# Linear attention and a gated mixture of attention experts on one core: the same steps in another listed order

## The chip, the core and the metric

The kernel runs on one core of a Trainium2 chip, in one launch. The metric is the device time of an execution in microseconds (us), the median of three runs. A core has a matrix engine (TensorE, PE in the profile; its weight loads stand under PEld), VectorE (DVE), ScalarE (ACT) and GpSimd (POOL), each with its own queue in order, and SyncE (SP), whose queue issues most of the loads and stores. SBUF is the core's working memory of 128 partitions; matmuls write to PSUM, of which this kernel uses eight banks of 128 x 512 elements.

## The reference

```python
def phi(x):
    proj = np.einsum('bhsd,df->bhsf', x, w_phi)
    proj = proj - np.max(np.abs(proj), axis=-1, keepdims=True)
    return np.concatenate([np.exp(proj), np.exp(-proj)], axis=-1)
q_p, k_p = (phi(q), phi(k))
kv = np.einsum('bhsf,bhsd->bhfd', k_p, v)
z = np.sum(k_p, axis=2)
num = np.einsum('bhsf,bhfd->bhsd', q_p, kv)
den = np.einsum('bhsf,bhf->bhs', q_p, z)[..., None] + 1e-06
x = num / den                     # then (batch, 576, 512), heads side by side
...
logits = x @ w_gate               # 4 experts, the best 2 of each row weighted by a softmax
for e in range(4):
    q, k, v = x @ wq[e], x @ wk[e], x @ wv[e]
    a = softmax(0.125 * q @ k.T, causal)
    out += weight_e * (a @ v @ wo[e])
```

There are 8 batches of 8 heads, 576 rows, 64 columns a head and 128 features. The second part is a causal attention of 576 rows for each batch and expert.

## The kernel before, in words

The work is cut into steps. Generators stand for streams: loads of k, q and v (`load_k`, `load_q`, `load_v`), projections of keys and queries of the 32 pairs of heads (`stream_k`, `stream_q`, matmuls of L499), their features (`phi_k`, `phi_q`), the sums over keys (`stream_kv`: L591 and L599 for the last 64 rows, L624 for kv, L635 for z), numerators and denominators (`stream_n`: L721 and L732), and for each batch the projections (L295), scores (L852), gates (`gates`), row maxima (`maxima`), sums of scores (`sums`, L1019), weighted values (L1048) and the output projection (L295 again). A step that copies from PSUM may go to ScalarE (L304) or to VectorE (L316).

Matmuls use the array in shapes: 128x128 (L295, L646), 64x128 (L499, L852), 64x64 (a part of L852), 64x32 (L591, L599) and 128x32 (L624, L635, L721, L732, L1019, L1048, L942).

The order is written out. `ORDER` (L72) is a string with one character a step: it names the place, in the list of live streams, of the stream that takes its next step. `SIDES` (L104) has one digit for each step that may go to either of two engines, 0 for ScalarE and 1 for VectorE. `Plan.loop` (L226) reads both:

```python
for c in ORDER:
    s = self.streams[ord(c) - 48]
    st = s[1]
    assert st.pred is None or st.pred()
    if isinstance(st.eng, tuple):
        st.eng = st.eng[int(next(sides))]
```

A step issues its instructions when it is taken, so this one string sets the order in every engine's queue, in SP's queue of loads and in GpSimd's. A step that needs a PSUM bank takes the free bank that was last used earliest. `in_order` (L246) ties each instruction to the one before it on its engine, and lets each GpSimd reduction or mask (L694, L977, L960) wait for the last VectorE operation listed ahead of it that works in SBUF alone.

Three helpers matter here. `phi_q` (L689) has GpSimd find the largest absolute value over 128 partitions (L694, `mx` from `u`), which VectorE then subtracts (L696). `maxima` (L963) does the same for scores (L977), and VectorE subtracts it from the scores (L981). `key_sum` (L570) has GpSimd issue a transfer that adds in SBUF (L332, from `ek` to `zs`, 512 KB), after which VectorE adds two halves (L574) and TensorE sums them (L635). `keep_warm` (L457) issues rounds of three small matmuls on a tile `warm` at the start until the first row block of x is there.

Of the kernel before, what the change touches and what calls it, by code (L numbers as in the profile page):

```python
# [69 lines left out]


ORDER = (  # L72
    r'10000030084C0009CD9247DC26FBGB98BB0935E708GFG=HDB84DCH010HKDJGGHB0G0BG2EE=990=CBI5=BBD=7B::JE>2DHCC:4463=7988B'
    r'B=GGBJDD9::EGEE=>ELD=IH5:>21BJJEDE>HGD99=CCGHICFEB=G7J:H:ABH5425468FJ<IIE<0A<C;E@<<BFDGGF@EA;6DEEBFD@D7A;0HDE7'
    r'7JEDEDG6H9;;D99B8:F@B979G9C>AGFE99808E17A:?2AF@59H3CIJ6CEFB99LCL0IHFFJFG::H4>>>>96877D9FJ=EB8@FBBIBB=GBGB>8B6?'
    r'>EA;;5;;FGF;JDD@EAF?88E3=F012;C88:ECEDD8@6;5;=>B=?B8BBB999AEDID7BA6EBD=IHDA7;GH8DFC@;;;6IDJ;@H;HMJIHHB;EG;CCB?'
    r'FFFFGCFB18H08038F48G88;5HAGFAA=;;:CL>?8CCECBAAKCBB@:::B:9AGJC<EHG99HFF=A?DDDIEJ@BCC883228888D::I6P88GFKHINBF83'
    r'NGMA@77?NA5FE31?I@CKFD<99>>9KK<=KAKC8884820HKEKFI=E8GHA6=<DE987FF>B976G7>7I88I=<E=DAHD2<88888=5J9GALC<032KHBBJ'
    r'HA8?6L<LK0IKGBAF899=@77=H==BKDA:::<JJIOF>:N<<DIFAIIH::CLMDIIKH8;HEJJ;CEH:CI:LGC6;GF8H:IL5FKG8:::KGL@OQPN88IO::'
    r':MMM?J=M:A>L>AIK4MMKIKFFF?J882K>IJ=JE0IEE;G;HF<DE<<G?FHFGF=F@IC<:8M8;:5BGGIDHHCDFJEE<8IICHIC=BLIKMDHMC::JPOI:9'  # L80
    r'MPO<GRHHBFFPPP999JH6<D18EEGAF8J>FC<7F0CEIE@D38DFD83@@KCC@I>GG8BBHF;;BIH<E7C>CFG2DE8BBD?C==8DC>88B>==9;9=97KI7L'
    r'JI=F=FF8B5OG68OEOGB>E8888KLA9BL9M79F?LAGIKM8JJ54IJAIHJ8H6H<38=1@82887?G=BFB::::EJ6F:MDK=DEFAK:J<?F@8806C@??ACD'
    r'FF:AFGF988897GF?DAEDA>CDC7@@GDE2:G:C5KG:B@DCB8M@:J=EOA::N:088834230?IFHJFJI@I:IF=:H?GG=I=ABECD;98I88;EGH6E=AGG'
    r'EBED8D6C::DC::HCC:EDLGGIMMM<CDJ<@<KBBS=<<O?DNA9AFKRDOC;HEG99JDCBFJ?GAABI<K=J?883E??EG?E7GFF@GHG@FB@F79F=9H1ACM'
    r'CAGG<E5D888HAG2CAFF7I7888=@3>IDFF8D<E<8EEF<8<BCE<>G56889M>PQ8DCJHN8K>LLK>HK99;D9;IJ0JGHJD8GI@GG?EEEGF8E577:HK<'
    r'FFE<FH6FE>0::::8D88142C8M6EC?<CDEDG@K::FLHDA8893IBF@9EJFJ8AHE>D8FF87HF7I:CGJFDGDB:L::K:5LHJFAAGQ6@I>GF8JF=MMHI'
    r'K>A88D:EE:JE=AAF;:08==EI@D@@CGC8<ECGG8;;9JG8EE8DH:CIFFE>=H><G:<:5BEH:DCGF:>O6OE:<<HB2HGD@ANK<9A=KO@IP<M06GO93C'
    r'A1842883MF9EDBMHM888>88MIIH8KEK>AG9989IG=A8FJH8K7F78LL7L6HH8C>PHIQ=NHGCFKF23AKG8999NIE;H?K7B<HH5B=7IAHEEMJG4EI'
    r'I708IAE@:GG>DB<D8FB:B::NNG66:KFLL::K3@B8210828588KH9BJJILI=CABD9G78GJ7IJ6AF=B8HJ8LAMFGGLH=5<K<KJA8J==L=JA==E<D'
    r'DQIHO83880<P<<<;NHS;:BSHHGN8O8HMKN8NHHA:>:D:G=KGPFOB?OO:OKHLLIGGA:@NG:::;8<EKGNM6I?>MJKH>?FF;6K=IIIHGF;:FGFF8:'  # L90
    r'=I:9LCKEAB::FKLLFCD5JTE<RRRIDLFD<ETB<QQ10C4<DCNDCHEGCGC=MJCD<0QLQMHBF@EHCJ@9FE<9823GD88F@@I@HCC@GB88E<E888BECD'
    r'?HB;98HC<><>7@EBFABF5F76FEEELHF99481H@EIH>J@>@@DGHH9J6@FC6IF;;77KHN<LIH83J8888GEF989<HF8F<288@839@GG@HFCFH077K'
    r'JBI>CA28A<H858CCC<68:II::B:NELHHIJIACCHID:6IICE:89HE98FF5HC?GFGF@BFFGF7=::KJJG::M::LIKELPHH7H8F<FCNC<<>OOGOO0H'
    r'GFHJ:::;8:8F?J8?@MJ??KL>DDDH2=38GJGCDFDFF;;88;5FFH8<HKLKBHCB>CC6<EF<=@@DFDCH<C<BB:=??D?9EDFFFCJF::?FJGHEIIHH:G'
    r':AAEPG9NUD=NF9=C?FKF9G7QPD1737016NPMJNPDOPN?AF?77ICCE>?LDD16055GI5?J9H;<<?=AB5@<=A=AE3<2<E?666555GF=FD<50DHI:G'
    r'C<G;E;FE:9851?BB7558D?D@A54A2>AB@A4??4A3C12?A?>=2C==2C244EE6<222D654446I@BEH4=>=CF0007607020=CFDCD?0224459:=<0'
    r'B22A9=H112>I>@AF<ID080=C224C220@E9@>?0B88577<06:?7<:>59<:19::69:>99B?=8A9:2>3=0>:395;<:<7:9777445444085?=>=0<<'
    r'2<52;>7C6C99916@611000022?0@?87559A3A=5?3@C8=58:84:;;00<656670=888?6@88<7>;;=7=9:0;;6<<03<<9628488366442223:30'
    r'0000052258;;5:<32811:78:7796301000:2997:0>@55855509896598001005:7:;68757577;57515766655315005005846440:3B5@;5?'
    r'3;:=<1:8751715::2146464755444151211411143463311048518832223=;63229883717100817555667055651210010<=413<<<0<00::'  # L100
    r'52912855552200543010'
)

SIDES = (  # L104
    r'10000000111000000000000011000010000011000011000000010000000000000100100100000001000000000010000000000000000000'
    r'00000000010000001100000100000000000000000000000000000000000000000100001001000000000000110000000000000000000000'
    r'00001000000000000000010100000010100010000100000101000000110000000100000000000000010000001000010000000001000000'
    r'00010010110000000000101001000000000000000000000000010000001000110000000000011000000000011100000000100110101010'
    r'00100000100000000000000011000000000000010000000100000000001000000000000010110101'
)  # L110


# [1060 lines left out]
```

## Time and profile before

| | |
|---|---|
| median of 3 runs | 599.58 us (599.35 to 599.69) |
| the profiled execution | 600.02 us |
| its span, first to last instruction | 598.2 us |
| busy: TensorE, VectorE, ScalarE, GpSimd | 582.6, 542.5, 452.0, 276.9 us |

The span is the profiled execution's own time without what lies around the first and the last instruction, 1.8 us. A busy time is the time in which at least one instruction of that engine ran. Matmuls overlap each other, so a busy TensorE need not be one at its peak.

### The profile page before, as it was taken

To read this page: it belongs to the slowest core of one execution; us is meant where nothing else is said; L and a number is where in the kernel's file an instruction comes from. 1 tells how busy PE (TensorE), PEld (TensorE's weight loads), DVE (VectorE), ACT (ScalarE), POOL (GpSimd) and SP (SyncE) were. 2 spreads that over 40 slices of the span, in tenths; PEclk is the share of its full clock that TensorE was granted. 3 is DMA by queue.
4 is the path that set the end of the run, shared out by engine and by line. 5 is a ranking of instruction groups with operands and counts; after the bars stand their busy time and mean duration, and the time that the engine had idled before them with its cause. 6 is when DMAs were issued, how large, how long until landed. Compare 5 with 4: busy or idle time off the path is not lost.

```text
span 598.2 us, 19532 instructions
## 1 busy us (share of the span) xinstructions
PE 582.6 (97%) x7909; PEld 448.3 (75%) x7909; DVE 542.5 (91%) x1155; ACT 452.0 (76%) x1104; POOL 276.9 (46%) x195
## 2 busy tenths in 40 slices
PE   8999999999999999999899999999999999999986
PEld 6665888578875788767686787975887678778875
DVE  6899999899999989889799989999999999997894
ACT  4999969877798978868578668776879777677552
POOL 3564661186535484265521457407553746231420
PEclk9999999999999999999999999999999999999999
DMA  8758255663065572355446552446325643111013
GB/s 210 187 151 182 49 125 139 151 136 84 28 159 129 125 183 60 109 118 159 110 105 149 112 138 84 115 110 171 109 45 119 161 101 88 29 55 41 1 42 118
DMA packets 55369, 67.13 MB, mean 112 GB/s; under 512 B 23664, under 2 KB 31216, under 8 KB 55280
## 3 DMA queue, kind: packets, MB, share of 16 engines
q1 hardware_dynamic: 47344, 50.62, 29.6%
q0 software_dynamic: 7616, 14.68, 14.7%
q8 instruction: 62, 1.02, 0.7%
q10 hardware_dynamic: 320, 0.59, 0.4%
q14 instruction: 27, 0.22, 0.1%
HBM read 36.64 MB, written 14.55 MB: 86 GB/s over the span
## 4 chain that ended last, share of the span: by engine, by line
PE 75%; DVE 14%; ACT 4%; DMA 3%; issue 2%; POOL 1%; SPq 1%; ACTq 0%; DVEq 0%; POOLq 0%
PE ps_c L295 28%; PE ps_c L499 11%; PE ps_c L732 9%; PE ps_c L624 7%; PE ps_c L852 5%; PE ps_c L721 4%; PE ps_c L1048 4%; DVE s L981 2%; DVE top L973 2%; DVE max L993 2%; PE ps_c L591 1%; PE ps_c L635 1%; DMA q_in<-in_qt_dram 1%; DVE pmax L562 1%; DVE u L696 1%
## 5 line engine op out<-in xcount | busy, mean ns | idle before, releaser
L694 POOL PARTITION_ALL_REDUCE mx<-u x64 | 147.5, 2336 | 71.8 <-ACT u L304 14.2
L295 PE MATMUL ps_c<-x,qk 128*128 128x256 f32 (+1 forms) x768 | 107.6, 299 | 1.5 <-DVE ek L565 1.3
L295 PEld LDWEIGHTS ps_c<-x,qk 128*128 128x128 f32 x768 | 102.9, 190 | 6.4 <-issue 1.7
L960 POOL TENSOR_SCALAR_AFFINE_SELECT s<-s 128x256 f32<-128x256 f32 (+1 forms) x80 | 42.5, 562 | 94.3 <-ACT s L304 17.9
L977 POOL PARTITION_ALL_REDUCE max<-top x16 | 57.4, 3590 | 56.2 <-DVE top L973 19.3
L306 ACT ACTIVATE ek<-ek 128x1024 f32<-128x1024 f32 x64 | 67.8, 1059 | 5.5 <-DVE ek L565 4.8
L332 POOL DMA_DIRECT2D zs<-ek x28 | 34.3, 1224 | 75.5 <-DVE pmax L562 15.6
L981 DVE TENSOR_TENSOR s<-s,max 128x1152 f32<-128x1152 f32 (+4 forms) x80 | 66.6, 867 | 1.5 <-POOL max L977 1.4
L306 ACT ACTIVATE s<-s 128x640 f32<-128x640 f32 (+4 forms) x80 | 57.2, 739 | 6.4 <-DVE s L981 6.1
L624 PE MATMUL ps_c<-ek,v_in 128*32 128x256 f32 x1024 | 61.7, 381 | 0.0
L304 ACT COPY s<-ps_c 128x320 f32<-128x320 f32 (+4 forms) x140 | 52.6, 432 | 10.9 <-PE ps_c L852 10.2
L304 ACT COPY u<-ps_c 128x320 f32<-128x320 f32 (+1 forms) x110 | 40.4, 401 | 18.3 <-PE ps_c L499 18.0
L295 PE MATMUL ps_c<-yh,wo 128*128 128x320 f32 (+1 forms) x256 | 52.9, 300 | 0.0
L295 PE MATMUL ps_c<-vg,x 128*128 128x260 f32 x384 | 49.8, 289 | 0.2 <-DVE ql L805 0.2
L696 DVE TENSOR_TENSOR u<-u,mx 128x576 f32<-128x576 f32 x64 | 50.0, 793 | 0.0
L295 PEld LDWEIGHTS ps_c<-vg,x 128*128 128x128 f32 x384 | 48.0, 192 | 1.0 <-DVE ql L805 0.4
L624 PEld LDWEIGHTS ps_c<-ek,v_in 128*32 128x32 f32 x1024 | 31.5, 110 | 21.8 <-issue 2.2
L562 DVE TENSOR_REDUCE pmax<-ps_c 128x4 f32<-128x512 f32 x64 | 42.7, 676 | 5.5 <-PE ps_c L499 5.1
L306 ACT ACTIVATE mx<-u 128x576 f32<-128x576 f32 x64 | 43.1, 683 | 5.9 <-DVE u L696 5.7
L1048 PE MATMUL ps_c<-s,vs 128*32 128x320 f32 (+4 forms) x896 | 47.1, 357 | 0.0
L499 PE MATMUL ps_c<-q_in,wf 64*128 64x256 f32 (+1 forms) x256 | 44.0, 436 | 1.0 <-DMA q_in<-in_qt_dram 1.0
L732 PE MATMUL ps_c<-mx,kv 128*32 128x320 f32 (+1 forms) x512 | 43.4, 410 | 0.5 <-ACT u L304 0.3
(131 smaller groups left out, 1334.1 us busy)
## 6 DMA issues: line engine op xcount, KB each, us to landing
zs<-ek POOLq DMA_DIRECT2D x28, 512.0 KB, 6.2
out_dram<-ot SPq DMA_DIRECT2D x32, 288.0 KB, 2.2
q_in<-in_qt_dram SPq DMA_DIRECT2D x60, 144.0 KB, 3.9
k_in<-in_kt_dram SPq DMA_DIRECT2D x64, 128.0 KB, 3.9
v_in<-in_v_dram SPq DMA_DIRECT2D x32, 256.0 KB, 3.6
kvd<-kvt SPq DMA_DIRECT2D x104, 48.0 KB, 2.0
kv<-kvd SPq DMA_DIRECT2D x26, 192.0 KB, 2.8
vt_in<-in_v_dram SPq DMA_DIRECT2D x16, 128.0 KB, 3.4
```

Source lines behind the costliest of these rows:

```text
L295: nc.tensor.matmul(o, a, b, start=start, stop=stop, skip_group_check=True)
L304: nc.scalar.copy(o, i)
L306: nc.scalar.activation(o, i, func, **kw)
L499: nc.tensor.matmul(o, a, b, start=True, stop=True, skip_group_check=True)
L562: dve(512, [mk], [pk]).tensor_reduce(out=m[:, us], in_=src, axis=AX.X, op=ALU.max, apply_absolute_value=True)
L624: nc.tensor.matmul(o[g, 0:2], v_in[:, 4 * h + t, k:64:2], ek[:, :, 2 * TURN[t] + h, :].rearrange("p c (w f) -> p c w f", w=4), start=False ...
L694: nc.gpsimd.partition_all_reduce(M, U, 128, bass_isa.ReduceOp.absmax)
L696: dve(S, [uk], [mk], port=True).tensor_tensor(out=U, in0=U, in1=M, op=ALU.subtract)
L732: nc.tensor.matmul(ps[g:g + 32, 0:n], kvi[:, 2 * k + (h ^ p % 2), 32 * c:32 * c + 32], P_[h][c][:, s0:s1], start=c == 0, stop=c == 1, skip ...
L977: nc.gpsimd.partition_all_reduce(big.rearrange("p e s -> p (e s)"), top.rearrange("p e s -> p (e s)"), 128, bass_isa.ReduceOp.max)
L981: dve(2 * (S - 128 * j), [('d', x, j)], [('max', z)], 1.11, True).tensor_tensor(out=block(s_, j, None, rows(j)), in0=block(s_, j, None, ro ...
L1048: nc.tensor.matmul(ps[r:r + 32, q0 - s0:s1 - s0], vs[:, j, 128 * g + 64 * e + k:128 * g + 64 * e + 64:2], ss[x][:, e, o + q0:o + s1], star ...
```

## The change

`ORDER` and `SIDES` are other strings; not a line of code is different. The new list has three steps fewer, all three rounds of warm-up matmuls. The same transfers, tiles and other instructions are issued, in another order on every engine, and some copies from PSUM are on the other of their two engines.

```diff
 ORDER = (
-    r'10000030084C0009CD9247DC26FBGB98BB0935E708GFG=HDB84DCH010HKDJGGHB0G0BG2EE=990=CBI5=BBD=7B::JE>2DHCC:4463=7988B'
...
+    r'11030400000008929424D7FCBCCECC00EFE09BDE653E507E9CD8HHEG8D99D2KD=D=8BFG2EG4:=K7JFM==GKLJ:64BDECBEH=BBB97EFF8BD'
...
 SIDES = (
-    r'10000000111000000000000011000010000011000011000000010000000000000100100100000001000000000010000000000000000000'
...
+    r'10000100000110001010010000000000000100000101000010011000000000100000011100000001000000000000000000000000000000'
...
```

**First listing.** TensorE, early in the program, around the sum over z (L635, from `zs`) of a pair of heads. `ps_c` are PSUM banks. Before:

```order
L599 MATMUL ps_c_63<-ekt,ones 32x4x32
L624 MATMUL ps_c_67<-ek_108,v_in_106 32x2x4x32 x16
L635 MATMUL ps_c_67<-zs,ones 32x4x32 x4
L499 MATMUL ps_c_69<-q_in_104,wf 128x320
L499 MATMUL ps_c_66<-q_in_104,wf 128x320
L721 MATMUL ps_c_65<-mx_139,kv_119 32x288
L721 MATMUL ps_c_65<-mx_140,kv_119 32x288
```

and in the change:

```order
L599 MATMUL ps_c_66<-ekt,ones 32x4x32
L624 MATMUL ps_c_67<-ek_108,v_in_106 32x2x4x32 x16
L635 MATMUL ps_c_67<-zs,ones 32x4x32 x4
L721 MATMUL ps_c_65<-mx_139,kv_119 32x288
L721 MATMUL ps_c_65<-mx_140,kv_119 32x288
```

Before, two projections (L499, 64x128) stand between the sum over z and the denominators (L721, from `mx` and `kv`), which have the same shape, 128x32. In the change the denominators follow at once.

**Second listing.** VectorE, where the row maxima of a block of scores (`s`, `max`) are subtracted (L981). GpSimd's steps stand in the same written list: before, a transfer L332 ahead of the first row here, and one reduction L694 each ahead of the fourth, the sixth and the seventh row; in the change the transfer just ahead of the first row's step, and three reductions in one go ahead of the fourth row (the first L562). Before:

```order
L299 TENSOR_TENSOR x_146<-ps_c_65,x_146 128x256
L316 CAST yh_171<-ps_c_70 128x256
L765 TENSOR_TENSOR ps_c_68<-ps_c_68,xf 128x320
L299 TENSOR_TENSOR yl_172<-ps_c_70,yh_171 128x256
L981 TENSOR_TENSOR s_154<-s_154,max_156 128x2x576
L299 TENSOR_TENSOR x_146<-ps_c_68,x_146 128x320
L981 TENSOR_TENSOR s_154<-s_154,max_156 128x2x448
L562 TENSOR_REDUCE pmax_123<-ps_c_63 128x4
L565 TENSOR_TENSOR ek_109<-ps_c_63,pmax_123 128x4x128
```

and in the change:

```order
L765 TENSOR_TENSOR ps_c_63<-ps_c_63,xf 128x320
L696 TENSOR_TENSOR u_130<-u_130,mx_138 128x576
L299 TENSOR_TENSOR x_146<-ps_c_63,x_146 128x320
L562 TENSOR_REDUCE pmax_123<-ps_c_66 128x4
L565 TENSOR_TENSOR ek_109<-ps_c_66,pmax_123 128x4x128
L316 COPY u_131<-ps_c_68 128x256
L752 RECIPROCAL facd_163<-facd_163 128x18
L981 TENSOR_TENSOR s_154<-s_154,max_156 128x2x576
L562 TENSOR_REDUCE pmax_123<-ps_c_70 128x4
L565 TENSOR_TENSOR ek_109<-ps_c_70,pmax_123 128x4x128
```

L981 of 128x2x576 was listed right behind the last part of an output's evacuation (`yl`), between two reductions on GpSimd. Now a maximum and a subtraction for the keys' features (`pmax`, `ek`), a copy of `u` and a reciprocal stand between the reductions and L981.

**Third listing.** VectorE in the last batch, behind the subtractions of one block's maxima (L981) and ahead of the gates (from L915 on). `top` holds the running maxima (L973) that the last GpSimd reduction reads; L993 are the sums of the block before. Before:

```order
L316 COPY s_154<-ps_c_66 128x448
L316 COPY s_154<-ps_c_66 64x64
L993 TENSOR_TENSOR max_156<-s_153 128x2x448
L993 TENSOR_TENSOR max_156<-max_156,s_153 128x2x320
L973 TENSOR_TENSOR top_155<-s_154 128x2x448
L993 TENSOR_TENSOR max_156<-max_156,s_153 128x2x192
L973 TENSOR_TENSOR top_155<-top_155,s_154 128x2x320
L993 TENSOR_TENSOR max_156<-max_156,s_153 64x2x64
L973 TENSOR_TENSOR top_155<-top_155,s_154 128x2x192
L973 TENSOR_TENSOR top_155<-top_155,s_154 64x2x64
L743 STREAM_TRANSPOSE widey_142<-ps_c_70 128x288
L316 COPY vs<-ps_c_67 128x260
```

and in the change:

```order
L316 COPY s_154<-ps_c_68 128x256
L993 TENSOR_TENSOR max_156<-s_153 128x2x448
L993 TENSOR_TENSOR max_156<-max_156,s_153 128x2x320
L993 TENSOR_TENSOR max_156<-max_156,s_153 128x2x192
L973 TENSOR_TENSOR top_155<-s_154 128x2x448
L993 TENSOR_TENSOR max_156<-max_156,s_153 64x2x64
L973 TENSOR_TENSOR top_155<-top_155,s_154 128x2x320
L973 TENSOR_TENSOR top_155<-top_155,s_154 128x2x192
L973 TENSOR_TENSOR top_155<-top_155,s_154 64x2x64
L299 TENSOR_TENSOR yl_174<-ps_c_63,yh_173 128x320
L743 STREAM_TRANSPOSE widey_142<-ps_c_64 128x288
L829 TENSOR_TENSOR vs<-ps_c_65,vs 64x260
```

The two copies of scores (`s_154`, 448 columns and 64 rows of 64) have become one of 256 columns, and the copy of `vs` is no longer there; ScalarE has these copies now.

## Rows read from the trace of the kernel before

**Rows 1.** The page of the kernel before, span and part 1, and the clock by core.

```profile
span 598.2 us, 19532 instructions
PE 582.6 (97%) x7909; PEld 448.3 (75%) x7909; DVE 542.5 (91%) x1155; ACT 452.0 (76%) x1104; POOL 276.9 (46%) x195
...
core 0: 598.2 us, clock 0.997
```

**Rows 2.** The page, part 4: the chain that ended last, shares of the span.

```profile
PE 75%; DVE 14%; ACT 4%; DMA 3%; issue 2%; POOL 1%; SPq 1%; ACTq 0%; DVEq 0%; POOLq 0%
```

**Rows 3.** TensorE's waits: line, what ended them; us in total, times, longest.

```profile
PE ps_c L635 <- DVE zs L574: 1.8, 1, 1.8
PE ps_c L1019 <- DVE max L993: 1.5, 2, 1.2
PE ps_c L295 <- DVE ek L565: 1.3, 1, 1.3
...
PE ps_c L499 <- DMA q_in<-in_qt_dram: 1.0, 1, 1.0
...
PE ps_c L721 <- DMA kv<-kvd: 0.6, 1, 0.6
```

**Rows 4.** Timeline of TensorE, the end: start, us, instruction, [idle before <-releaser].

```profile
583.24 0.40 PE L1019 MATMUL ps_c<-max,ones 128*32 128x224 f32 x4 [1.20 <-DVE max L993]
...
593.31 0.31 PE L295 MATMUL ps_c<-yl,wo 128*128 128x320 f32 x1
```

**Rows 5.** Timeline of TensorE, the start.

```profile
1.06 2.10 PE L295 MATMUL ps_c<-warm 128*128 128x128 bf16 x18 [1.06 <-DVE col L339]
4.00 0.80 PE L499 MATMUL ps_c<-wf,kt_in 64*128 64x128 f32 x4 [0.84 <-DMA kt_in<-in_kt_dram]
```

**Rows 6.** The chain in order of time, two stretches: start, us, what.

```profile
54.62 2.08 PE ps_c L732 x32
56.70 1.73 PE ps_c L624 x32
...
319.36 2.18 PE ps_c L499 x15
321.54 1.87 PE ps_c L624 x32
```

**Rows 7.** Timeline of GpSimd and VectorE: a reduction beside L755, and L755 alone.

```profile
441.85 2.15 POOL L694 PARTITION_ALL_REDUCE mx<-u  x1 [4.99 <-DVE facy L752]
441.89 1.29 DVE L755 TENSOR_TENSOR facy<-facy,gc 128x18 f32<-128x18 f32 x1
...
292.84 0.17 DVE L755 TENSOR_TENSOR facy<-facy,gc 128x18 f32<-128x18 f32 x1
```

**Rows 8.** Timeline around 415 us, and L981 by form (xcount | busy, mean ns).

```profile
411.48 1.23 POOL L332 DMA_DIRECT2D zs<-ek  x1 [0.47 <-ACT ek L306]
412.25 7.08 POOL L694 PARTITION_ALL_REDUCE mx<-u  x3
...
412.19 3.02 DVE L981 TENSOR_TENSOR s<-s,max 128x1152 f32<-128x1152 f32 x1
...
418.69 0.41 PE L295 MATMUL ps_c<-x,qk 128*128 128x320 f32 x1 [1.33 <-DVE ek L565]
...
L981 DVE TENSOR_TENSOR s<-s,max 128x1152 f32<-128x1152 f32 x16 | 23.1, 1443 | 1.5 <-POOL max L977 1.4
```

**Rows 9.** Groups by form: xcount | busy us, mean ns of one | idle before, releaser.

```profile
L562 DVE TENSOR_REDUCE pmax<-ps_c 128x4 f32<-128x512 f32 x64 | 42.7, 676 | 5.5 <-PE ps_c L499 5.1
L316 DVE COPY u<-ps_c 128x256 f32<-128x256 f32 x7 | 2.8, 406 | 1.5 <-PE ps_c L499 1.5
...
L306 ACT ACTIVATE ek<-ek 128x1024 f32<-128x1024 f32 x64 | 67.8, 1059 | 5.5 <-DVE ek L565 4.8
```

**Rows 10.** The z transfers: duration ns min/median/max, first to last start; time to landing.

```profile
L332 POOL DMA_DIRECT2D zs<-ek x28: 1200/1220/1369, 42.5 to 505.0; - x28
...
DMA to landing us min/median/max: 5.1/6.2/7.4
```

More of the change, by code (lines that the diff above doesn't have):

```diff
@@ L78 @@
[L78 to L82, printed above, removed]
@@ new lines @@
+    r'9B=C>=8EFE=5KE:JFIGCI>>F:DB>:IHHHG9D=:B=HJEI:9BHG2G=HG378C:GHGG540;;C@D1<<<A@E;::9EE5IFHBC6HEE8DGGG4D;DAEK@GH;'
+    r'A7;<<AF:F7G@298;GC:CC::;EGEF9:CCCA30E::88FBB116F9>AHE7EC>>D?>>HGDH@E@DE4::3C9>B78E@8753:E9@0GB9421BBBCIHCBBCCB'
+    r'0C5E;;8;;=;HI;;8J?@F>IHCECD8=@A9FC>>CB886DDCBC8CD5;C9EADEABB=8D=C97F7AFH0IGG=;C;AA;HE>688A832J;JH>;I;;;GE88JFI'
+    r'H=FEBEEAABF?EG8DFFE@D;;5:C?D;?43L0A8@DA:=ED:DHAE@F@F@F@::::<HG6:?A999E8882308AQCBFDGD18?CNO8KFAMB688LKELABFLF8'
+    r'KHKIH@@HAH99@@<7EHBF56GF7>>481I888089E2=H==3CEBIE8=D=GG77KIH=AAG?=FC9988?95882HJA7876B=?MMK?FMGKL@HA288HEE86FL'
@@ new lines @@
+    r'?FLEE<IA99LKEGJIDI<H877><43<J>GIG<<IAD=:EII:F::::GJ8DKMLJ@<;AG;KAH8HC:::F?EOKK::KIHALLLFF5=J8QFFQ?>ALKEHMK::JG'
+    r'88I288::JHJJI:;@KFF1IIF0IGL?>K=>@L?G6D;;LHIH<<EHG<@KDDDF>EC88H::5=GGDBBHEEEGBBGB<BB<EFANJFJ?F?A:;BGB8=GDHII::9'
+    r'HDBTKIMGJGCJNNN9@GJ699BEEMGBB@@@ED?DHDFCCCB@HEBBAA088803FE@HE888;;I3C=D<FF8FF=8AC@C899=7>87=888DDD;7I2=HGC=E5='
+    r'BD7M9MC<68HII<8MOOHGK<J@@I@C99DMBNC798NO7NDLCC=JDIID6EJG?601324888:5D@D3KL:<::F::CMFMJEMKLIE@J88G8HJ8F6AJGII88'
+    r'C8HB9G9HHHH:7G7CHGI?H::NKC:JM:CBMC:EALG@ML5PIJJI:K::KBEAJH:JKBFH88813?6BG;J:;G=248C88GF@BKLIJ>FFH2D>AFE9@E>E8E'
@@ new lines @@
+    r':F8D:C::@FIEFMLFLKBABBBBJ<<D<<C>FLICKPK?OC<MH>DKKLJC999F0773<8BDD<GHDG?MKEE8HI<088?GHACD8G?6?KG@@JJFJ9B9JEBBEC'
+    r'@HJ75NLC<CBIJ8AHF=G?8H8HHHG8B9HA6;57OHGEI04D88818IA>G>?E?EL8M<I<=L299;;<@8CLMKA?KEABKJIAH@9BD8G778D@@66EI<<E::'
+    r'5IG@B0?<C::I?JN:CCJHGDLMNBLF:CBDE998=ICBI32JE7J3K8888H7I>88830:JHEKI>G::HFD8:IMMI:5O88DDBK6D:HCKCFK8QJGG8G=LI8'
+    r'0GHACH:HIC=FIG:?C:E:GGCCF>ALK=>I@E;8<;;F29KFFD8GKG6E8FH<@G<FEEBEHCHGH:<:ED:BDJH5LHMD::F<NMA=NPP<AJC9K9GOG888C<'
+    r'<82406813KKN?L<9P?8K8IIHNJA8N8NI9DA948LAF8K97L7DOK7N8MLB6CFR<JRDJKB8KNN>I288C99LCKF>BDJ<5EDIJ7F6CEK6JEE897GEKF'
@@ new lines @@
+    r'=DDG87:5:DM@@B@D::3<PP@PGMF8288FEEL:1>LE9@@=9=F7JKM7JFI@::=KF<JH8HGACF8038N==M?MN8I8D56H8?=PPNMHF?AO@E=O=J<;<0'
+    r'G<Q<QCF<JHP>HF<;I;8=KG:JLKO:QGLG88JKLE8GI83G8>JG:HIHL:JLG:LJ:K:::GIA?FDHIIF8:JL=JGEG9=GHFFFEHGHFF;;=;<>FD:;:GK'
+    r'MGG8GG5:LGC6H@DM:BNDLD?EF<<FDJJ@L6GE<DRJ<PD=NJGDLJL=GI?JAAIE<K9AG9I9IAHJFK@IJ3@G8@I888A<I2240GKB1DIDG@0<=EJ8J>'
+    r'8F88?BCDCA?AE>BB68GGFC1E577>G99DI9L@6AF6FI>D882@JI@>8884DIHH@F;;7IBGG>I7EFFJ898JBH<F<C9EFC897@@I73?DDACDC858F8'
+    r'BCCKA?K@HGCDC8028386C<GGIC::::::CFJIKEIA<JF88IBGE98G9FH5:HFHG87EFGFKJG8>00821779H993:HABJ5<LJ96EMQC;;;EFLP99CL'
@@ new lines @@
+    r'FMGLA9EGF999EAHH<@H=H7KLJHEEH@>IH5EDHG<@GCFCF::774HFHKG;;;=>F<<F?D=?>I>G;H8?@H>AHDE>9>AHHA;:@EJD>=CHJ??99G;;EH'
+    r'>I<@D@98L@KLLJGBD>88DON06?H>55LNGJ:M<IDED?<DAGA6GCG<<?61@066E1J05AA5B5>>5G:E;23G69C99F6DG@965E:FC59E9F9:9GA9DE'
+    r'E985CEE66G8D9<50GHEGGCECEAABA@5565@4BBCA4C14880011G9111<>=@9<7GC15<53333333=?JBJ?H?0A0FFEEBD000:=02=:0?A@2>=52'
+    r'2?D?6411;:@5CBE6C?:007060:AA6D><9B?;>;>222A222=08:<:;>;:<:A@35>:9689:<;89:0331=;=?<4:64;:7:;755:896668598444>='
+    r'=8<0072222<;19<D;87A1169FA:7C;7CEDC766C<9:9;@=:@>485000<808805:00607;>>=<<59==;0346017789387487677643444002222'
@@ L102 @@
+    r'0095=>8:32:00011==33;93;4:68500589785501028788899988550000877557759075975:51076661660055655555<<77:009@@68;?;8'
+    r'67:41711179>69;;86610114544414111111244339861424341:4528927398232155515100203335443354330061>6321=0=<0;;;01915'
+    r'22254424036303200'
 )
 SIDES = (
-    r'10000000111000000000000011000010000011000011000000010000000000000100100100000001000000000010000000000000000000'
-    r'00000000010000001100000100000000000000000000000000000000000000000100001001000000000000110000000000000000000000'
@@ L107 @@
[L107 to L109 removed]
+    r'10000100000110001010010000000000000100000101000010011000000000100000011100000001000000000000000000000000000000'
+    r'00000100000000000000000000001000000000000000000000000000000100001000100100100000000000000000010000000000000000'
@@ L110 @@
+    r'00001000001000000100000000001010010010100000000000000000000000000100000000000000000000001000010000011100100010'
+    r'00100000001000000001000100100010000000100000000000100000000000000100100010000000000000100001010000010000000000'
+    r'00000000000000001100001100000000001000100010010000000000000000000000000010101010'
 )
```

23 lines of the change are left out of this document (removed).

## Prediction, made before the change was run

> **What bounds the kernel now.** I read the engines' busy shares first, then the chain of waits, then the waits of TensorE alone. TensorE is busy 582.6 of 598.2 us, VectorE 542.5, ScalarE 452.0; the mean granted clock is 0.997, so TensorE is at its upper level, 2.4 GHz, all the way [rows 1]. The chain that ended last is TensorE for 75% and VectorE for 14% [rows 2]. So TensorE's stream bounds the span, and an order can change two things in it: how often the array changes its shape, and how often it stands still. Of its 598.2 - 582.6 = 15.6 us of idle time, 1.1 pass before the first matmul [rows 5] and 598.2 - 593.6 = 4.6 behind the last one, while the last copies and stores run [rows 4]. Some 9.9 us are left. The longest of these waits are in [rows 3] and [rows 5]: VectorE ends 1.8, 1.5 (two waits) and 1.3 us of them, loads 1.0, 0.8 and 0.6. A new order cannot win more than those 9.9 us by removing waits; what it can lose by making new ones has no such limit.
>
> **The start.** Both programs issue the same instructions but for the warm-up matmuls, which come in rounds of three: 51 before, 42 in the change. In the start 18 of them take 2.10 us, and the first projection then waits 0.84 us for its load [rows 5]. The change lists 27 there: 27 x 0.117 = 3.15 us, to 4.21 us, where the projection started at 4.00. So 0.2 us is lost at worst, and nine times 0.117, 1.05 us, gained at best. I take nothing: what covers them is the wait for loads and for the copies behind these projections, and without that cover they would cost their 1.05 us.
>
> **Changes of shape.** Counted over the whole listing, the array's shape changes 222 times before and 213 times in the change, nine fewer (the first listing above shows how). The price is in pieces of the chain: the 32 matmuls of L624 take 1.73 us right behind L732, which has their shape, and 1.87 behind L499, which has another [rows 6]. That is 0.14 us a change, on the bounding engine: 9 x 0.14 = **1.26 us less**. The rows are read to 0.01 us, so the ends are 1.2 and 1.35.
>
> **GpSimd's holds on VectorE.** VectorE's L755 takes 0.17 us alone and 1.29 when it starts 0.04 us behind a GpSimd reduction (L694): 1.12 us held [rows 7]. The largest loss of this kind stands behind a transfer. At 411.48 GpSimd issues the z transfer (L332, 1.23 us), reductions queue up behind it, and the subtraction L981 of 128x1152 elements, which takes 1.44 us on average, takes 3.02. So VectorE comes late to the subtraction L565, which gives back a PSUM bank, and TensorE waits 1.33 us for that bank [rows 8]. This is the place of the second listing: in the change a maximum, a subtraction from PSUM, a copy and a reciprocal stand between these reductions and L981. The maximum takes 0.68 us and the copy 0.41 [rows 9]; with the other two that is more than one hold of 1.12. I take this wait as gone: **1.33 us less**. The ends are 0, since a second reduction of the same queue can meet L981 as the first did, and 1.6, what it lost to the hold (3.02 - 1.44).
>
> Over the program, the next GpSimd operation is listed at most two VectorE instructions behind a transfer seven times before and twice in the change, and a reduction L694 has at most one VectorE instruction between it and one whose inputs are all in SBUF 16 times before and 10 times now. Six holds of 1.12 us are 6.7 us of VectorE's time. VectorE is not the bound: what TensorE sees of this is part of its waits in [rows 3]. So I count nothing beyond the one place, and keep 2 us for the range.
>
> On this the Trainium skill (SBUF — State Buffer, "SBUF: two separate sides") says that VectorE and GpSimd share one pair of SBUF ports under an exclusive lock, which the one that starts first keeps for its whole instruction. By that L755 in [rows 7] would have waited until the reduction's end, 2.15 us; it ended 1.33 us after the reduction began, so the trace shows a shorter hold. By the rule six holds would be worth 12.9 us of VectorE's time; the sum stands on the measured hold.
>
> **Sides.** Eleven copies net pass from VectorE to ScalarE. A copy of `u` of 256 columns takes VectorE 0.41 us [rows 9], so it has some 4.5 us less to do, and ScalarE about as much more. By load neither reaches TensorE, and I take 0; what ScalarE's longer queue can cost is rival 3.
>
> **The end.** TensorE's work behind the last scores is the same in both listings. In the third listing VectorE has one copy of scores ahead of the last row maxima where two stood, and one copy of `vs` less ahead of the gates; these copies pass to ScalarE, which has to be done before the same maxima. TensorE waits 1.20 us for the last sum of scores [rows 4], so the ends are 1.2 less and, where ScalarE carries the chain, one copy of 0.4 more. I take 0, between the two.
>
> **Loads and the rest.** SP's queue is in order, and the loads in it change places as well: the load of q for which TensorE waited 1.0 us, and the way of a kv block through memory, 0.6 us [rows 3], have other neighbours now. Every other wait of [rows 3] is undone in its old place and can come back in another. I take them as redrawn with the same sum; the ends are all of some 9 us gone, and as much again.
>
> **Sum.** The profiled execution took 600.02 us, the span and 1.8 us around it. 600.02 - 1.26 - 1.33 = 597.4. The median of the runs is 599.58, 0.44 below the profiled one, so I predict **597.0 us**. About 0.2%, 1.2 us, is what a measurement of this kernel can tell from no change.
>
> **Rivals.**
> 1. The redrawn waits sum to just what is saved, 2 to 3 us more: 599.5, no difference. For it: every wait of [rows 3] is under 2 us, so two or three pairs listed a microsecond too close do it. Against it: fewer changes of shape stay saved whatever is late. Chance 0.24.
> 2. More waits go, because VectorE is 4.5 us lighter and held less often: half of the 9 us. 599.58 - 1.26 - 4.5 = 593.8. For it: VectorE ends the three largest entries of [rows 3]. Against it: each is undone only by what stands ahead of it, not by a lower load. Chance 0.12.
> 3. Slower: ScalarE gives PSUM banks back late. Eleven more copies queue there behind exponentials of 1.06 us [rows 9], and a late bank costs TensorE what it cost at 418.69, 1.33 us [rows 8], or a little less, 1.2. It decides from three such new waits on; with four, 4 x 1.2 - 2.6 = 2.2 us more: 601.8. For it: one such exponential is about as long as the waits of [rows 3]. Against it: it is idle for 24% [rows 1]. Chance 0.20.
> 4. The z transfers land later. In the change 17 transfers have at most one VectorE instruction between them and one that works in SBUF alone, before 11. The issue takes 1.20 to 1.37 us, the landing 5.1 to 7.4 [rows 10]. Six transfers 2.3 us later, of which TensorE sees 1.8 us twice, as once in [rows 3], are 3.6 - 2.6 = 1.0 us more: 600.6. The Trainium skill (SBUF — State Buffer, "SBUF: two separate sides") speaks for this one: while VectorE runs a two-port operation GpSimd cannot write a transfer's descriptors, and the transfer waits. In [rows 10] the issue varies by 0.17 us, so this trace does not bear it out. Chance 0.05.
> 5. The new list does not reach the engines. Against it: all three listings differ. I give it nothing.
>
> **How the numbers follow.** The forecast has 0.39; its own range is 595.5 to 598.3. With rival 2, faster by over 0.2% has 0.51. Rival 1 and 0.02 of rival 4 lie within 0.2%, 0.26; slower has rival 3 and the rest of rival 4, 0.23. The range takes in rival 2 below and rival 3 above, with 0.6 us beyond each for redrawn waits: 593.2 to 602.4.
>
> **What would show it.** Right: no wait of TensorE over a microsecond for L565, and subtractions of 128x1152 below 1.44 us on average; TensorE's waits for VectorE down by 1 us or more in sum; VectorE's busy time near 537 us. Wrong: new waits of TensorE for ScalarE or for loads of a microsecond each, VectorE's busy time not below 541 us, or more than 1.3 us of waiting ahead of the last L1019.

## The result and the profile after

The change runs in 590.01 us (median of 6 runs, 588.5 to 593.92) where the kernel before took 599.63 beside it (596.44 to 601.66): a ratio of 0.9852, 95% interval 0.981 to 0.9893. That is 9.6 us less, where 2.6 less were predicted; it lies below the range given. The direction was right, the size and most of its sources were not.

The page of the change, span and part 1, and the shares of the chain that ended last, as [rows 1, 2]:

```profile
span 586.7 us, 19535 instructions
PE 575.4 (98%) x7900; PEld 444.3 (76%) x7900; DVE 532.0 (91%) x1144; ACT 454.9 (78%) x1115; POOL 276.5 (47%) x195
...
PE 91%; DVE 4%; DMA 2%; ACT 2%; issue 1%; SPq 0%; DVEq 0%
```

TensorE was 75% of the chain and is 91% now; VectorE fell from 14% to 4%. VectorE is busy for 10.5 us less. Note TensorE's own busy time: it fell by 7.2 us, though only nine short warm-up matmuls are gone. Part of these 7.2 us is TensorE's clock, as the table below and the last section show.

TensorE's waits in the change, as [rows 3] (line, what ended them; us in total, times, longest):

```profile
PE ps_c L1019 <- DVE max L993: 2.0, 1, 2.0
PE ps_c L942 <- DVE col L933: 1.6, 1, 1.6
PE ps_c L295 <- DVE col L339: 1.1, 1, 1.1
PE ps_c L499 <- ACT u L304: 0.6, 1, 0.6
PE ps_c L721 <- DMA kv<-kvd: 0.4, 1, 0.4
...
PE ps_c L635 <- DVE zs L574: 0.2, 1, 0.2
```

Between the first matmul (the wait on L339) and the end nothing over 0.6 us is left. The waits for `zs` (1.8), for L565 (1.3) and for q (1.0) are gone. The end is worse: 1.6 and 2.0 us, where [rows 4] have 1.20.

The subtraction L981 of 128x1152, by form, as [rows 8] (xcount | busy us, mean ns of one):

```profile
L981 DVE TENSOR_TENSOR s<-s,max 128x1152 f32<-128x1152 f32 x16 | 21.5, 1346 | 0.0
```

It was 1443 ns on average. Both signs that the prediction named for its term of the hold are there; of its signs for the contrary there is one, more than 1.3 us ahead of the last L1019.

To see where along the run the time went, I took the start of every 300th matmul (warm-up ones left out) in each trace, and the time between them. Worked out in this way, in us:

```
matmul number       0-300  300-900  900-1800  1800-3900  3900-4200  4200-5400  5400-5700  5700-7200  7200-last
starts, before at       4       28        67        133        286        313        401        423        534
before              23.61    39.40     65.81     153.33      27.07      87.33      22.90     110.19      59.66
the change          20.95    39.66     63.70     153.11      23.53      86.25      21.12     108.89      60.33
h2_old_tail         21.09    39.69     63.70     152.95      23.53      86.22      21.12     108.84      58.10
a2_first            21.43    39.64     63.70     152.86      25.52      87.33      22.90     111.12      59.64
a3_second           24.15    39.40     64.37     153.51      23.53      86.33      21.12     108.80      58.10
g1_sub_late         24.21    39.40     65.37     153.91      25.54      87.33      22.69     111.55      59.65
s1_order            22.29    47.44     64.24     155.52      23.53      88.13      22.01     109.98      61.39
s3_sides_start      22.31    47.45     64.08     153.02      23.53      86.30      21.12     109.12      60.31
s4_start_banks      22.70    47.63     64.21     153.01      23.53      86.37      21.12     108.81      60.92
p_half_before       23.75    39.40     65.77     154.15      24.63      85.84      21.75     109.38      59.66
p_half_after        22.74    39.99     63.70     152.98      23.53      86.06      21.12     108.92      60.91
```

(The other names are the experiments below.) Many stretches repeat to 0.02 us in every kernel that has the same listing there. Others vary by a microsecond and more between executions of one listing, where a load is waited for or where TensorE's clock falls. From matmul 3900 on before took 27.07 us in its own profile, and 25.54 in g1_sub_late, which has the same listing there and the same wait for `zs`. The difference is the granted clock, which is at 0.50 for 3.3 us in before's profile and at 1.00 in the other (busy times by windows: us, then TensorE, weight loads, VectorE, ScalarE, GpSimd; clock, DMA share, GB/s). Before, and below it g1_sub_late:

```profile
290.00:297.50 7.50, 5.68 (x100) 3.49 (x91) 5.72 (x13) 5.21 (x12) 1.23 (x2) 1.00 0.35 95
297.60:300.90 3.30, 3.30 (x17) 3.30 (x16) 3.05 (x9) 2.71 (x10) 2.31 (x1) 0.50 0.19 51
```

```profile
291.00:298.50 7.50, 5.69 (x100) 3.50 (x91) 5.73 (x13) 5.22 (x12) 1.23 (x2) 1.00 0.33 90
298.60:301.90 3.30, 3.30 (x29) 3.30 (x28) 3.30 (x9) 2.89 (x9) 2.30 (x1) 1.00 0.22 60
```

So 1.5 us of what the two profiles differ by are the clock and not the listing. The change's gain lies at the start (2.7 us), around matmuls 900 to 1800 (up to 2.1), 3900 to 4200 (2.0, and 3.5 with the clock), 5400 to 5700 (1.8), and in smaller pieces; the end gives 0.7 us back.

### The profile page after: what moved, and what is told of

It reads as the page before. It is cut to its first block, busy times and chain, and to the rows that moved or that the text cites. A ratio compares the mean times of both kernels' runs of the same rounds, so it can differ in the third digit from the quotient of the medians.

```text
span 586.7 us, 19535 instructions
## 1 busy us (share of the span) xinstructions
PE 575.4 (98%) x7900; PEld 444.3 (76%) x7900; DVE 532.0 (91%) x1144; ACT 454.9 (78%) x1115; POOL 276.5 (47%) x195
## 4 chain that ended last, share of the span: by engine, by line
PE 91%; DVE 4%; DMA 2%; ACT 2%; issue 1%; SPq 0%; DVEq 0%
PE ps_c L295 36%; PE ps_c L499 11%; PE ps_c L732 10%; PE ps_c L624 8%; PE ps_c L1048 8%; PE ps_c L852 7%; PE ps_c L721 5%; PE ps_c L1019 1%; PE ps_c L591 1%; PE ps_c L635 1%; DMA zs<-ek 1%; DMA kv<-kvd 1%; PE ps_c L599 1%; ACT ek L306 1%; DVE s L981 1%
## 5 line engine op out<-in xcount | busy, mean ns | idle before, releaser
L694 POOL PARTITION_ALL_REDUCE mx<-u x64 | 147.0, 2322 | 68.1 <-DVE zs L574 15.8
L981 DVE TENSOR_TENSOR s<-s,max 128x1152 f32<-128x1152 f32 (+4 forms) x80 | 65.2, 852 | 0.0
L332 POOL DMA_DIRECT2D zs<-ek x28 | 34.2, 1223 | 59.4 <-ACT ek L306 21.2
L304 ACT COPY s<-ps_c 128x448 f32<-128x448 f32 (+4 forms) x138 | 51.2, 430 | 12.0 <-PE ps_c L852 11.3
L304 ACT COPY u<-ps_c 128x256 f32<-128x256 f32 (+1 forms) x118 | 42.8, 401 | 19.3 <-PE ps_c L499 19.0
L295 PE MATMUL ps_c<-yh,wo 128*128 128x256 f32 (+1 forms) x256 | 52.7, 300 | 0.0
L562 DVE TENSOR_REDUCE pmax<-ps_c 128x4 f32<-128x512 f32 x64 | 42.5, 682 | 4.7 <-PE ps_c L499 4.2
L306 ACT ACTIVATE u<-u 128x576 f32<-128x576 f32 x64 | 43.4, 686 | 0.3
```

Source lines behind the costliest of these rows:

```text
L295: nc.tensor.matmul(o, a, b, start=start, stop=stop, skip_group_check=True)
L304: nc.scalar.copy(o, i)
L306: nc.scalar.activation(o, i, func, **kw)
L562: dve(512, [mk], [pk]).tensor_reduce(out=m[:, us], in_=src, axis=AX.X, op=ALU.max, apply_absolute_value=True)
L694: nc.gpsimd.partition_all_reduce(M, U, 128, bass_isa.ReduceOp.absmax)
L981: dve(2 * (S - 128 * j), [('d', x, j)], [('max', z)], 1.11, True).tensor_tensor(out=block(s_, j, None, rows(j)), in0=block(s_, j, None, ro ...
```

## Experiments

The medians of before beside these runs lie between 598.76 and 599.66 us.

**Order and sides apart.** Two kernels take the written order of one listing and the sides of the other; 113 of 520 sides differ.

```diff
 s1_order:  ORDER of the change
-SIDES of the change
+SIDES of the kernel before, step by step
 s2_sides:  ORDER of the kernel before
-SIDES of the kernel before
+SIDES of the change, step by step
```

> The change's order with the sides (VectorE or ScalarE) of the kernel before: 113 of 520 copies and other two-sided steps change engine against the change, none against before. Theory order (the gain is TensorE's waits that the new order removes all along the program): 589 to 592 us, within 0.4% of the change. Rival sides (VectorE's lighter load carries it): only the nine changes of shape and the start remain, 595 to 598.

> The order of the kernel before with the change's sides. Theory order: 598 to 601 us, no better than before (or worse, since these sides were drawn for another order). Rival sides: 591 to 594, and TensorE's waits for VectorE clearly fewer than in rows 3.

Measured: s1_order 606.44 us, ratio 1.0125 (1.0102 to 1.0147); s2_sides 620.28, ratio 1.0349 (1.0327 to 1.037). Both theories fall: neither half carries the gain. The new order with the old sides is 16 us slower than the change, the new sides in the old order are 21 us slower than before. VectorE's busy time in the two (page, part 1):

```profile
PE 583.3 (97%) x7900; PEld 447.3 (74%) x7900; DVE 533.9 (88%) x1155; ACT 453.9 (75%) x1104; POOL 277.0 (46%) x195
```

```profile
PE 588.1 (95%) x7909; PEld 450.7 (73%) x7909; DVE 545.3 (88%) x1144; ACT 454.9 (73%) x1115; POOL 276.3 (45%) x195
```

The first is s1_order, the second s2_sides. With before's sides and the new order VectorE is already down to 533.9, so 8.6 of its 10.5 us come with the order; the copies that moved away take off another 1.9 in the new order, and in the old one the same move adds 2.8. And s2_sides issues the very matmuls of before, yet TensorE's busy time is 588.1 against 582.6 [rows 1]. Some 1.4 of these 5.5 us are the clock, an estimate: TensorE worked 6.1 us at a granted clock of 0.50 in s2_sides (from 567.6 to 574.3 us) and 3.3 in before, and at half the clock half of that is lost. The other 4 us are spread over the run, in the same matmuls in the same order, where the clock reads 1.00 in both. What differs there is when their inputs and banks are free, so a busy time of TensorE seems to hold waits that no idle gap shows; this is argued from the busy times, no run takes it apart.

**The end.** At step 2918 (matmuls up to about 550 us) both listings have done the same steps; there one can follow the other.

```diff
 h1_new_tail: steps 1 to 2918 as before
-the steps left as before
+the steps left in the change's order, with its sides
 h2_old_tail: steps 1 to 2918 of the change
-the steps left as in the change
+the steps left as before
```

> The kernel before up to its step 2918 (matmuls up to about 550 us), then the steps left in the change's order and sides; at this cut both listings have done the same steps. Between about 550 us and the end the change lost some 0.9 us against before in the two profiles. Theory (the gain lies ahead, the end gives a little back): 600.0 to 601.0 us, and 1.5 us or more of waiting ahead of the last L942 and L1019. Rival (the end costs nothing, the two profiles differ there by chance): 599.0 to 599.8.

> The change up to step 2918, then the steps left as in the kernel before. Theory: 588.5 to 589.5 us, some 0.9 below the change, and faster than both kernels; waits ahead of the last L942 and L1019 near 1.2 and 0.5 us instead of 1.6 and 2.0. Rival (the end costs nothing): 589.7 to 590.5.

Measured: h1_new_tail 602.08 us, ratio 1.0048 (1.003 to 1.0065), so the new end costs 2.9 there; h2_old_tail **587.22**, ratio 0.9813 (0.979 to 0.9836), 2.8 below the change's median. The theory holds, at three times its size. That h2_old_tail beats the change rests on the last column of the table (58.10 against 60.33, and 58.10 again in a3_second), since the intervals of the two ratios overlap. The cause is in the timelines of VectorE and GpSimd (start us, us, instruction, [idle before <-releaser]). The change:

```profile
557.12 1.09 DVE L973 TENSOR_TENSOR top<-s 128x896 f32<-128x896 f32 x1 [3.64 <-ACT s L304]
...
560.30 3.58 POOL L977 PARTITION_ALL_REDUCE max<-top  x1 [1.01 <-PE ps_c L295]
```

```profile
556.37 0.38 ACT L304 COPY vs<-ps_c 128x260 f32<-128x260 f32 x1 [2.20 <-PE ps_c L295]
556.64 0.38 ACT L304 COPY s<-ps_c 128x256 f32<-128x256 f32 x1
```

and h2_old_tail:

```profile
554.30 1.09 DVE L973 TENSOR_TENSOR top<-s 128x896 f32<-128x896 f32 x1 [0.79 <-ACT s L304]
...
557.78 3.58 POOL L977 PARTITION_ALL_REDUCE max<-top  x1 [3.37 <-DVE top L973]
```

In the change a copy of the last scores stands on ScalarE behind a copy of `vs` that waits 2.20 us for TensorE. VectorE waits 3.64 us for it, and the last GpSimd reduction starts 2.5 us later. Part of the 2.8 and 2.9 us by the medians may again be the clock: behind the new end's wait of 2.0 us h1_new_tail's profile has 0.50 from 571.8 to 575.1 us and s4_start_banks's (below, the same end) from 570.4 to 573.7, while the old end kept 1.00 in before and in h2_old_tail. The change's own profile kept 1.00 there too, so the 2.2 us of the table (60.33 against 58.10) are without it.

**Single edits in the kernel before.** Three edits, each at a wait that the prediction names, and all together.

```diff
 w1_warm27
+three rounds of warm-up matmuls (9)
 first projection (L499, from kt_in)
-three rounds of warm-up matmuls (9)
 q's projection
 z1_add_early
+L574 zs
 L758 rb
 L973 top, L973 top
-L574 zs
 g1_sub_late
-L981 128x1152, L981 128x896
 L562 pmax
 L565 ek
+L981 128x1152, L981 128x896
```

> The kernel before with one edit: the nine warm-up matmuls listed between the first projection and q's are listed ahead of it, so that 27 stand there as in the change and not 18. Count unchanged. In the profile of before, the warm-up matmuls behind the wait of 0.84 us still start every 107 ns, later ones every 56 ns, and q's eight matmuls take 2.02 us where the change's take 1.24. Theory (the longer warm-up brings TensorE to its upper level before the projections): q's eight take 1.2 to 1.3 us, the first k projection starts 1.7 to 2.0 us earlier, and 1 to 2.2 us of that last to the end: 597.2 to 598.4 beside before's 599.4. Rival (loads and copies hold the next projections anyway): same early lead, but less than 0.5 us left at 28 us; 599.0 to 599.6.

> The kernel before with VectorE's one addition for the key sums (L574, near 295 us) listed three VectorE steps earlier, ahead of L758 and two maxima L973. Theory (waits are local, each undone by what stands ahead of it, and what is saved stays saved): the wait of 1.8 us for it goes, TensorE is 1.5 to 1.9 us earlier from there on, 597.5 to 598.0 beside 599.4. Rival (VectorE's next work is as much later and another wait takes its place): below 0.5 us left 20 us later; 599.0 to 599.9.

> The kernel before with the two subtractions L981 of one block (1152 and 896 elements, near 412 us) listed behind the next maximum L562 and subtraction L565. The prediction's term for the hold: the wait of 1.33 us for L565 near 418.7 goes and nothing else changes, 598.0 to 598.3 beside 599.4. Rival (the hold moves with L981, or the exponentials behind it come late and TensorE waits for them): less than 0.5 us gained, 599.0 or more.

> The three edits together: 27 warm-up matmuls first, L574 early, the two L981 late; nothing else of the change. Theory (local waits that add up): the sum of the three single gains, 3.5 to 5.5 us, 594 to 596, that is about half of what the change gains. Rival (what one edit saves is waited for at the next place): less than 2 us, 597.5 or more.

Measured: w1_warm27 598.84 us, ratio 1.0002 (0.9986 to 1.0018); z1_add_early 598.73, 1.0009 (0.9997 to 1.0022); g1_sub_late 600.06, 1.0028 (1.0014 to 1.0043); all3 598.19, 0.9986 (0.9972 to 1.0). None of the three gains anything alone, and g1_sub_late loses 1.3 us. The rival is right in all four (in w1_warm27 even the early lead stayed out, see the last section; it and z1_add_early lie 0.2 to 0.3 us below the rival's range, as the kernel before did beside them, with 598.76 where 599.4 had been assumed). In z1_add_early and g1_sub_late the traces show why: a wait that is undone alone comes back next door. TensorE in z1_add_early, where the sum over `zs` no longer waits:

```profile
294.43 0.40 PE L635 MATMUL ps_c<-zs,ones 128*32 128x128 f32 x8
295.83 2.02 PE L295 MATMUL ps_c<-x,qk 128*128 128x320 f32 x12 [0.99 <-DVE ql L805]
```

and VectorE and TensorE in g1_sub_late, where the first L565 now runs ahead of L981, and the second one is late instead:

```profile
413.90 0.69 DVE L565 TENSOR_TENSOR ek<-ps_c,pmax 128x512 f32<-128x512 f32 x1
414.50 4.39 DVE L981 TENSOR_TENSOR s<-s,max 128x1152 f32<-128x1152 f32 x2
...
420.40 0.69 DVE L565 TENSOR_TENSOR ek<-ps_c,pmax 128x512 f32<-128x512 f32 x1
```

```profile
421.14 2.02 PE L295 MATMUL ps_c<-x,qk 128*128 128x320 f32 x12 [1.35 <-DVE ek L565]
```

VectorE stands still for at most 0.1 us at a time in either of these pieces; whatever goes first, something else is late.

**Stretches.** The change's listing in one part of the run alone, with its sides; the end always as before.

```diff
 a1_start:  before
-steps 1 to 284
+steps 1 to 284 of the change, then the steps left in the order of before
 a2_first:  the same with steps 1 to 1397
 a3_second: the same with steps 1398 to 2918
```

> The change's order and sides for its first 284 steps (to about 46 us), then what is left in the order and with the sides of the kernel before. Theory (a stretch keeps its time whatever follows it, so that gains of stretches add): 2.2 to 2.9 us ahead at 45 us and all of it kept, 596 to 597 beside before's 599. Rival (the gain is one of the whole listing; a lead is waited for at the seam or behind it): below 1 us left, 598 or more.

> The change for its first 1397 steps (to about 250 us), then before. Theory: the lead of 3.7 to 5.2 us that the change has there is kept, 594 to 595.5. Rival: below 2 us left, 597 or more.

> Before for its first 1397 steps, the change from there to step 2918 (about 550 us), the end again as in before: the other part of what h2_old_tail has of the change. Theory: the gain of the stretch from 250 to 550 us, 7 to 8.5 us, 590.5 to 592; with a2_first's gain it makes h2_old_tail's 12. Rival: less than 5 us, and the two do not add up to 12.

Measured: a1_start 598.45 us, ratio 0.9978 (0.9954 to 1.0002); a2_first 596.2, 0.9953 (0.9926 to 0.9979); a3_second 591.21, 0.9854 (0.9824 to 0.9884). a3_second is as the theory has it; a2_first lies between the two; a1_start, with 0.9 us of its lead left, is the rival's. The two halves win 3.2 and 8.2 us, together 11.4, where h2_old_tail wins 12.0: at this one cut, gains of whole stretches add. In a1_start's profile the lead of 2.7 us at the 300th matmul is there; 0.6 is lost at the seam, and further on, at 201 us, TensorE waits 1.2 us for a load (the other of the two waits here, 0.2 us, is at the start):

```profile
PE ps_c L499 <- DMA kt_in<-in_kt_dram: 1.4, 2, 1.2
```

**Where a side costs.** The change with before's sides in its first 420 steps, 25 of the 113.

```diff
 s3_sides_start: ORDER of the change
-SIDES of the change, steps 1 to 420
+SIDES of the kernel before, steps 1 to 420
```

> The change with the sides of the kernel before in its first 420 steps alone (to about 70 us): 25 steps differ from the change instead of 113. In s1_order the stretch from 17 to 67 us took 9 us longer than in the change. Theory (a side costs where it stands, since the step's place was chosen for that engine's queue): the same 8 to 10 us longer, nothing lost behind, 598 to 600. Rival (the loss is one of balance, 113 sides together): a quarter of s1_order's 16 us, 593 to 595.

Measured: 600.35 us, ratio 1.0007 (0.9988 to 1.0026), 10.3 above the change: 25 sides undo the whole gain. In the table most of the loss lies in matmuls 300 to 900, 47.45 us against 39.66, with s1_order's 47.44. The theory holds, 0.35 us above its range. The clock is not the cause: it is at 0.50 from 38.1 to 41.4 us in this profile, but at 1.00 in s4_start_banks (below, the same sides), whose stretch took 47.63. TensorE and VectorE there:

```profile
60.15 0.64 PE L732 MATMUL ps_c<-mx,kv 128*32 128x256 f32 x8 [1.57 <-DVE u L316]
```

```profile
57.46 0.42 DVE L299 TENSOR_TENSOR x<-ps_c,x 128x256 fp32r<-128x256 f32 x1 [1.84 <-ACT x L304]
57.80 1.23 DVE L299 TENSOR_TENSOR vg<-top,vg 128x1040 fp32r<-128x1040 f32 x1
58.95 0.75 DVE L696 TENSOR_TENSOR u<-u,mx 128x576 f32<-128x576 f32 x1
59.62 0.48 DVE L316 COPY u<-ps_c 128x320 f32<-128x320 f32 x1
```

This is one of the new waits there. The copy of `u` that gives the bank back is VectorE's here and was ScalarE's. It takes 0.48 us, but it stands behind an instruction that waited 1.84 and two more of 1.23 and 0.75. The change has no wait over 0.2 us between 17 and 70 us.

**Banks.** The planner gives a step the free PSUM bank whose last use ends first by its own reckoning, so other sides bring other banks. Here the banks are written into the listing.

```diff
-                slot = sorted(self.psum[st.tag], key=lambda kt: self.last.get(kt[0], (0.0, ''))[0])[:st.n]
+                want = [int(next(slots)) for _ in range(st.n)]
+                slot = [next(kt for kt in self.psum[st.tag] if kt[0][1] == i) for i in want]
```

> s3_sides_start (the change with 25 sides of the kernel before) with the PSUM banks of the change written into the listing. The planner gives each step the free bank whose last use ends earliest by its own reckoning, so other sides also gave 33 of 711 bank uses another user before them. Theory (the side itself costs: the copy stands behind the wrong work in its new engine's queue): 598 to 601 us as in s3_sides_start. Rival (the banks cost: a matmul gets a bank that is given back late): 590 to 593.

> s1_order (the change's order, all sides of the kernel before) with the change's banks; in s1_order 139 of 711 bank uses had another user before them. Theory sides: 603 to 607. Rival banks: 591 to 596.

> s2_sides (the order of the kernel before, the change's sides) with the banks of the kernel before; in s2_sides 123 of 711 bank uses had another user before them. Theory sides: 615 to 621. Rival banks: 599 to 605.

> The change, its order and its sides, with the banks of s3_sides_start: 33 of 711 bank uses have another user before them, nothing else differs. Theory sides: 589.5 to 591.5, as the change. Rival banks: 597 to 601.

Measured: s4_start_banks 600.04 us, ratio 1.0023 (1.0002 to 1.0043); s5_order_banks 618.68, 1.0344 (1.031 to 1.0378); s6_sides_banks 627.49, 1.0485 (1.0444 to 1.0526); b4_banks_only 592.06, 0.9898 (0.9862 to 0.9934). A side costs by itself: s4_start_banks has the change's banks and stays where s3_sides_start was. The banks of another choice of sides cost more still (s5_order_banks is 12 us above s1_order, s6_sides_banks 7 above s2_sides, both slower than either range): picking banks by the sides at hand makes a bad match milder, it does not cause it. By an estimate from the profiles some 3 of the 12 and 6 of the 7 us are a lower clock: TensorE worked 10.0 us at 0.50 in s5_order_banks and 3.3 in s1_order, 17.9 in s6_sides_banks and 6.1 in s2_sides, and half of that is lost. Other banks alone (b4_banks_only) are 2 us above the change by the medians, between the two ranges; the intervals of the two ratios overlap, so a cost of the banks alone is not shown.

**Holds.** GpSimd's reduction L694 over half its columns, in both listings; the maxima of the other half are left out.

```diff
-        nc.gpsimd.partition_all_reduce(M, U, 128, bass_isa.ReduceOp.absmax)
+        nc.gpsimd.partition_all_reduce(M[:, 0:S // 2], U[:, 0:S // 2], 128, bass_isa.ReduceOp.absmax)
...
-        dve(S, [uk], [mk], port=True).tensor_tensor(out=U, in0=U, in1=M, op=ALU.subtract)
+        dve(S, [uk], [mk], port=True).tensor_tensor(out=U.rearrange("p (a s) -> p a s", a=2), in0=U.rearrange("p (a s) -> p a s", a=2),
+            in1=M[:, 0:S // 2].unsqueeze(1).to_broadcast([128, 2, S // 2]), op=ALU.subtract)
```

> The kernel before with GpSimd's reduction L694 over 288 of its 576 columns and the subtraction L696 taking these maxima twice (the same number of elements): the maxima of the other half are left out, and nothing is listed otherwise. Theory (the holds of VectorE by GpSimd are what the new listing mainly saves): VectorE's time lost to holds falls from 17 us to 8 to 11, and TensorE gains half of what the change gains, 593 to 596. Rival (holds are taken up by VectorE's slack before TensorE sees them): 597.5 to 600.

> The change with the same halved reductions. Theory (holds): the change has fewer of them, so it gains less, 1 to 2.5 us, 587.5 to 589, and the gap between the two listings shrinks from 9.6 to 4 to 7. Rival: 589.5 to 591, and the gap stays at 8.5 or more.

Measured: p_half_before 595.12 us, ratio 0.9917 (0.9897 to 0.9938); p_half_after 589.9, 0.9836 (0.9816 to 0.9855). Halved reductions win 4.5 us for the kernel before and 0.1 for the change, which is the rival's value there (589.5 to 591). The gap between the two listings shrinks from 9.6 to 5.2, as the theory has it. So the holds are nearly half of the gain, 4.4 us, with some 3 us either way by the intervals of the ratios. Before with the halved reductions, page, part 1:

```profile
PE 579.5 (98%) x7909; PEld 445.9 (75%) x7909; DVE 535.5 (90%) x1155; ACT 451.5 (76%) x1104; POOL 217.5 (37%) x195
```

VectorE's busy time falls by 7.0 us with the same instructions, and TensorE's by 3.1, of which 1.5 are the fall of the clock that this profile does not have. In the table the gain lies in part where the change wins: 24.63 from matmul 3900 on (25.54 without the fall of the clock), 85.84 from 4200 on, 21.75 from 5400 on, and nothing up to matmul 1800. One reservation: a shorter reduction also delivers its maxima 0.9 us sooner. That was not taken apart from the hold itself.

## Why the prediction was wrong

- **The bound.** TensorE's stream does set the span. But "a new order cannot win more than those 9.9 us by removing waits" counted idle gaps alone. In the change's profile the idle time between the first and the last matmul, worked out as in the prediction, is 5.5 us, 4.4 less than the 9.9, and yet its last matmul starts 11.6 us sooner. Of the other 7.2 some 1.5 are the clock, and the nine warm-up matmuls and the changes of shape have a share; but s2_sides shows some 4 us more of busy time for the same matmuls, clock apart. What is waited inside the busy time lay outside the cap.
- **Holds: the step that failed first.** The place of the second listing was right; its wait is gone, and that stretch is 1.8 us shorter. "So I count nothing beyond the one place" was wrong: the two listings differ by 4.4 us in what the reductions cost them (3 us either way), not by 1.33. What the lost holds are worth to VectorE came out close to the 6.7 us that the prediction had for six: by an estimate from the traces (for each form of its instructions, the time above what a fifth of them stay within, where that is over 0.15 us) VectorE lost 16.3 us in before and 10.4 in the change and in s1_order. The step that failed is what TensorE sees of it. The reason given for zero, that VectorE is not the bound, is an average; in single stretches it is full. And the term hung on the wrong lever: moving L981 alone (g1_sub_late) brought nothing; the gain is there in a3_second, where the whole second half of the listing is the change's.
- **The start.** Priced at 0 between +0.2 and -1.05 as a matter of nine warm-up matmuls. The stretch to the 300th matmul is 2.7 us shorter in the change; moving the warm-up alone (w1_warm27) wins nothing. Alone in front of the old listing (a1_start) some 0.9 us of that remain. What makes the start shorter no run takes apart.
- **The clock.** "At its upper level, 2.4 GHz, all the way" came from a mean of 0.997. In the profile of before TensorE was at the lower level until 7.4 us, by the length of its matmuls, and again from 297.6 to 300.9 us, which cost it 1.5 us.
- **Sides.** "By load neither reaches TensorE" asked the wrong question. A copy of 0.5 us costs 1.6 where it stands behind the wrong work. VectorE's busy time was predicted near 537 and came to 532.0, and the order did most of it.
- **The end.** Taken as 0, with 0.4 us as the worst. It costs 2.2 us by the table and 2.8 by the medians. The mechanism had been named (copies pass to ScalarE, which must be done before the same maxima); its size came from the copy's own duration instead of from what stands ahead of it.
- **Loads and the rest, "redrawn with the same sum".** Between the start and the end the waits were not redrawn, they went. The nearest rival was the second one, 593.8, with "held less often" right; the copies made VectorE lighter by 1.9 us, not by 4.5. It was still 3.8 us too slow, and the end, which it did not price, worked against it. Rival 3, late copies on ScalarE, came true once, at the end.
- **Changes of shape.** No run changed them alone, so the 1.26 us stand untested.

The account, as far as it goes: holds 4.4 by the medians, the start 2.7 by the profiles (0.9 by a1_start's median), shape at most about 1.3, the end -2.2. Together that is 4.4 to 6.2 of the 9.6 us. These figures come from different measures, and their places may overlap, so it is no exact sum. The other 3 to 5 us stay open: no single run names what they are.

## What to carry to other kernels

When an order, the engines of its copies and its buffers were searched together, judge the change as one piece: compare it stretch by stretch between points where both listings have done the same work, and splice there, since here the gains of whole stretches added up, while three instructions moved singly gained nothing. Price a copy on another engine by the queue it joins, not by its duration or by that engine's load. And don't take idle gaps as the most that can be won on an engine whose instructions overlap; compare the busy time of the same instructions across runs instead, after a look at the granted clock of every stretch, since a mean of 0.997 can hide 3.3 us at half the clock.
